# Differences of two SBUF operands on VectorE instead of GpSimd, and weight preparation begun earlier, in a kernel of attention and two feed-forward networks

## The chip, the cores and the metric

One Trainium2 chip, one core of it. The engines are TensorE (PE, with its weight loads as PEld), VectorE (DVE), ScalarE (ACT), GpSimd (POOL) and SyncE (SP, which here issues all transfers). The metric is the device time of one execution in microseconds, as the median of several runs.

## The reference

Causal attention in a window of 128 positions (4 sequences of 576, 8 heads of 64, with a linear position bias), then two feed-forward networks (FFN) over all 2304 tokens, everything in float32:

```python
x = attention(q, k, v)                    # 2304 x 512
h = x @ w_in                              # 512 -> 2048, first FFN
y = (h / (1 + exp(-1.702 * h))) @ w_out   # 2048 -> 512
g = y @ w_gate                            # 512 -> 1536, second FFN
out = (g / (1 + exp(-g)) * (y @ w_val)) @ w_out2
```

The weights come as float64 (pairs of 32-bit words), which the kernel turns into float32 itself.

## The kernel before

**Split operands.** Each operand of a large matmul is held as two parts, a high part that ScalarE copies (to type float32r) and a low part, the difference of the original and the high part. Each product is three matmuls: high x high, high x low, low x high (`three`, and the inner loops of `product` and `o_part`). The low parts are what the change is about: every one of them is a subtraction of two SBUF operands, or in some places of PSUM and SBUF.

**First FFN.** The 18 tiles of 128 tokens form five blocks of 4, 2, 4, 4, 4 tiles. `seq` is the order of 80 steps (block j, slice f of 16): the first eight slices of block 0, all of block 1, the second half of block 0, then blocks 2, 3, 4. A step is `h_part` (12 matmuls into `hp`; ScalarE's tanh; VectorE's `th`, L584; ScalarE's copy `gh`; VectorE's difference `gl`, L592) and `y_part` of the step two before (`AHEAD = 2`; 12 matmuls). The attention of blocks 0 and 1 and the first eight steps follow a handwritten list (`PLAN`). The attention of blocks 2 to 4 runs beside the steps of the block before: scores on TensorE, exponentials on ScalarE, and on GpSimd `normalise` (L421) and two selections (L478, L481).

**Preparation.** The generator `preparation` turns the second FFN's weights into what its products read and stores them in scratch memory (`w_scratch`, `wo_scratch`). There are 36 units: for each of six pairs of feature slices, two of the gate, two of the value and two of the output weights. A gate or value unit takes eight steps: a load (`raw`), three VectorE instructions of 512 columns beside one of ScalarE (`fraction`, L217, L219, L223), four sums and differences of 128 columns (L271), and three calls of `halves` (L229 copies, L230 subtracts: `wa` twice with 256 columns, `wb` with 384), with two stores. An output unit takes four steps, one subtraction of 512 columns and one store. Loads, stores and buffers turn over one unit at a time. `advance(n)` adds n to an account and takes as many steps as it holds, each inside `issue_after` for the two marks, the latest ScalarE and VectorE instructions of the main work: the instructions of the step are queued behind these on their engines. It is called twice in each step of the first FFN with a pace that depends on the block, and once after each product of the second FFN.

**Second FFN.** The tokens form three superblocks of six tiles. Each of 18 periods q (superblock s, pair p) has 14 products of 384 columns (`gv_steps`: seven for the gate and seven for the value, a form of 2 x 2 block multiplication with seven products in place of eight) and six products of 512 columns (`o_part`) that read the gated result `p` of the period before. The seven operands of a superblock are differences of quarters of y, loaded from scratch memory (`yr`): `y_steps` makes them in four stretches, with seven calls of `split` (L650 copies, L651 subtracts, 768 columns) and four of `minus` (L655, 768 columns). In `gate`, VectorE makes `th` (L725, L726), ScalarE copies the high part of `p` (L728) and L729 subtracts; VectorE's sums `c` (L716) free TensorE's accumulators.

**Order.** Outside `PLAN` the order of instructions on each queue comes from a schedule made at build time with a model of durations; the `issue_after` hints are edges in it. On the chip each engine, and SP's queue of transfers, keeps that order.

Of the kernel before, what the change touches and what calls it, by code (L numbers as in the profile page):

```python
# [8 lines left out]
F32 = mybir.dt.float32  # L9
# [4 lines left out]
ALU = mybir.AluOpType  # L14
# [8 lines left out]
F0 = 8  # L23

CLOSE = 6

PACE = {2: 1.8, 3: 1.8, 4: 3.4}

PAUSE = 13

PACE_LATE = 0.7

O_SLOTS = 4

# [47 lines left out]
def attention_two_ffn(ctx: ExitStack, tc: tile.TileContext, q, k, v, w_in, w_out, w_gate, w_val, w_out2, yscr, wscr, woscr, out):  # L82
# [5 lines left out]
    nc = tc.nc  # L88
# [5 lines left out]
    NF1 = w_in.shape[0]  # L94
# [27 lines left out]
    def bank(name):  # L122
        return ps.tile([P, 512], F32, tag="b", name=name)
# [103 lines left out]

    def halves(t, at, src):
        nc.scalar.activation(out=t[:, at, 0, :], in_=src, func=AF.Copy)  # L229
        nc.gpsimd.tensor_tensor(out=t[:, at, 1, :], in0=src, in1=t[:, at, 0, :].bitcast(F32), op=ALU.subtract)  # L230

    def flat(t):
        return t.bitcast(F32).rearrange("p s r c -> p (s r c)")
# [332 lines left out]
    marks = {}  # L566
# [71 lines left out]
    def y_steps(s, tile_of):  # L638

        t0 = s * SUPER * P  # L640

        def quarter(i, j):
            t = yrp.tile([P, 2, HT], F32, tag="yr", name="yr")
            a = t0 + j * HT
            nc.sync.dma_start(out=t, in_=yscr[:, 2 * i : 2 * i + 2, a : a + HT])
            return t

        def split(c, src):
            t = tile_of(c)
            nc.scalar.activation(out=t[:, 0], in_=src, func=AF.Copy)  # L650
            nc.gpsimd.tensor_tensor(out=t[:, 1], in0=src, in1=t[:, 0].bitcast(F32), op=ALU.subtract)  # L651
            y2[s, c] = t

        def minus(out_, a, b):
            (nc.gpsimd if s else nc.vector).tensor_tensor(out=out_, in0=a, in1=b, op=ALU.subtract)  # L655

        b11, b12, b22 = quarter(0, 0), quarter(0, 1), quarter(1, 1)
        split(1, b11)
        minus(b11, b12, b11)
        minus(b12, b22, b12)  # L660
        split(5, b11)
        yield
        minus(b11, b22, b11)
        split(7, b12)
        b21 = quarter(1, 0)
        yield
        split(2, b21)
        split(6, b11)
        yield
        split(3, b22)  # L670
        minus(b11, b21, b11)
        split(4, b11)
        yield
# [16 lines left out]
    def product(q, m, i, bank_, start):  # L690
        half, at = W_OF[i]
        w, y = w2[q, m, half], y2[q // NP2, i]
        for kk in range(2):
            for n, (a, b) in enumerate(((0, 0), (0, 1), (1, 0))):
                nc.tensor.matmul(  # L695
                    out=bank_[:, :HT],
                    lhsT=w[:, kk, at, a, :],
                    rhs=y[:, b, kk, :],
                    start=start and kk == 0 and n == 0,
                    stop=kk == 1 and n == 2,  # L700
                    skip_group_check=True,
                )

    def gv_steps(q):

        banks, kept, c = {}, {}, {}
        p2[q] = [wpool.tile([P, 2, 2 * HT], F32R, tag=f"w{12 + 2 * (q % 2) + f}", name="p2") for f in range(2)]

        def keep_copy(m, i, b):
            t = pp.tile([P, HT], F32, tag="pc", name="pc", bufs=5)  # L710
            marks["a"] = nc.scalar.activation(out=t, in_=b[:, :HT], func=AF.Copy).ins
            kept[m, i] = t

        def add(m, i, b, k):
            t = pp.tile([P, HT], F32, tag="c2", name="c2", bufs=4)
            marks["d"] = nc.vector.tensor_tensor(out=t, in0=b[:, :HT], in1=kept[m, k], op=ALU.add).ins  # L716
            c[m, i] = t

        def gate(i):
            f, j = i  # L720
            g, v = c["G", i], c["V", i]
            at = slice(j * HT, (j + 1) * HT)
            th = pp.tile([P, HT], F32, tag="th2", name="th2", bufs=3)
            nc.scalar.activation(out=th, in_=g, func=AF.Tanh, scale=0.5)
            nc.vector.scalar_tensor_tensor(out=th, in0=th, scalar=1.0, in1=g, op0=ALU.add, op1=ALU.mult)  # L725
            nc.vector.tensor_tensor(out=th, in0=th, in1=v, op=ALU.mult)  # L726
            ph = p2[q][f]
            nc.scalar.activation(out=ph[:, 0, at], in_=th, func=AF.Copy)  # L728
            nc.gpsimd.tensor_tensor(out=ph[:, 1, at], in0=th, in1=ph[:, 0, at].bitcast(F32), op=ALU.subtract)  # L729

        def step(m, i):
            b = {1: "x", 6: "x", 7: "x", 4: "x", 2: "y", 5: "z", 3: "z"}[i]
            new = (m, b) not in banks
            if new:
                banks[m, b] = bank("s" + b)
            t = banks[m, b]
            product(q, m, i, t, new)
            if i in (1, 5, 6):
                keep_copy(m, i, t)
            elif i == 2:  # L740
                add(m, (0, 0), t, 1)
            elif i == 3:
                add(m, (0, 1), t, 6)
            elif i == 7:
                add(m, (1, 1), t, 5)
            else:
                c[m, (1, 0)] = t[:, :HT]
            if m == "V" and i in (2, 3, 7, 4):
                gate({2: (0, 0), 3: (0, 1), 7: (1, 1), 4: (1, 0)}[i])

        for pair in ((1, 5), (2, 6), (3,), (7,), (4,)):
            for m in "GV":
                for i in pair:
                    step(m, i)
                    yield m, i
# [119 lines left out]
    na = len(a_blocks)  # L875
# [52 lines left out]
    def preparation():  # L928
        raws = []

        def fetch_next():
            if len(raws) < len(todo):
                raws.append(fetch(slot, todo[len(raws)]))

        fetch_next()
        yield
        for i, u in enumerate(todo):
            yield from prepare(slot, raws[i], fetch_next, u)

    work, owed = preparation(), [0.0]  # L940

    def advance(n):
        owed[0] += n
        while owed[0] >= 1:
            owed[0] -= 1
            with ExitStack() as after:
                for ins in marks.values():
                    after.enter_context(tc.issue_after(ins))
                next(work, None)

    for idx, (j, f) in enumerate(seq):
        if idx < F0:
            continue
        if (j, f) == (1, 0):
            load_w1(NW1)
        if j < 2:
            need = f + 2
            if j == 1:
                need = max(need, F0 + (NF1 - F0) * (f + 1) // NF1)
            split_next(w1, raw1, need)  # L960
        if (j, f) == (na - 1, CLOSE):
            closed.append(True)
            attx.close()
            ya = bctx.enter_context(tc.tile_pool(name="ya", bufs=1, side="right", reuse_waits="tile"))
            yrp = bctx.enter_context(tc.tile_pool(name="yrp", bufs=3, side="right", reuse_waits="tile"))
            first = y_steps(0, lambda c: ya.tile([P, 2, 2, HT], F32R, tag=f"ya{c}", name="ya"))
        h_part(j, f)
        run(2 * idx)
        if (j, f) < (na - 1, PAUSE):
            advance(PACE.get(j, 0))  # L970
        if idx >= AHEAD:
            y_part(*seq[idx - AHEAD])
        run(2 * idx + 1)
        if (j, f) < (na - 1, PAUSE):
            advance(PACE.get(j, 0))
        if j == na - 1 and f > CLOSE and f % 2:
            next(first, None)
    for i in range(len(seq) - AHEAD, len(seq)):
        y_part(*seq[i])
    for m, half in (("G", 0), ("V", 0), ("G", 1), ("V", 1), ("O", 0)):  # L980
# [6 lines left out]
    pieces = {}  # L987
    for q in range(NQ):
        s, p = divmod(q, NP2)
        if s + 1 < NS and p == NP2 - 2:  # L990
            pool, tag = ((wpool, "w"), (ya, "ya"))[s % 2]
            base = (0, 1)[s % 2]
            pieces[s + 1] = y_steps(
                s + 1,
                lambda c, pool=pool, tag=tag: pool.tile(
                    [P, 2, 2, HT], F32R, tag=f"w{c - 1}" if tag == "w" else f"ya{c}", name="ya"
                ),
            )
        for n, (m, i) in enumerate(gv_steps(q)):
            if q or n > 5:  # L1000
                advance(PACE_LATE)
            if q > 0 and n == 11:
                o_part(q - 1, O_ORDER[0])
            if s + 1 in pieces and n % 6 == 5:
                next(pieces[s + 1], None)
            if q + 1 < NQ and i in (6, 4):
                load_weights(q + 1, m, 0 if i == 6 else 1)
        if q == NQ - 2:
            load_weights(NQ - 1, "O", 0)
        if q > 0:  # L1010
            for i in O_ORDER[1:]:
                o_part(q - 1, i)
            if q < NQ - 1:
                load_weights(q, "O", 0)
# [46 lines left out]
```

## Time and profile before

| | |
|---|---|
| median of 3 runs | 949.06 us (946.11 to 949.38) |
| profiled execution | 945.89 us |
| its span, first to last instruction | 944.2 us |
| granted TensorE clock | 0.992 of full speed |
| busy: TensorE, weight loads | 919.8, 787.9 us |
| busy: VectorE, ScalarE, GpSimd | 598.2, 422.0, 333.8 us |

Busy times are sums over the span of instructions' durations, overlaps counted once. Matmuls are pipelined, so a busy TensorE can still be below its full pace. On the span's axis the first FFN runs to about 520 us (block 2 from 207, block 3 from 315, block 4 from 425) and the second FFN from there.

### The profile page before, as it was taken

The numbers are of one execution on the slowest core, as the hardware profiler recorded it, in microseconds if no ns is written. First come the engines' busy times: TensorE is split into PE (matmuls) and PEld (weight loads), VectorE is DVE, ScalarE is ACT, GpSimd is POOL, SyncE is SP. The second block draws the span as 40 slices with busy tenths as digits, with TensorE's granted clock in tenths as the row PEclk, the third lists the DMA queues.
The fourth block names the chain that finished last, engine by engine and source line by source line (L and its number), as shares of the span: only waits on it lengthen the run. The fifth ranks groups of instructions, "written<-read, shape, count | busy, mean of one in ns | idle before, by whom it ended". The sixth has DMA issues, their size and how long they took to land.

```text
span 944.2 us, 15242 instructions
## 1 busy us (share of the span) xinstructions
PE 919.8 (97%) x5464; PEld 787.9 (83%) x5464; DVE 598.2 (63%) x1373; ACT 422.0 (45%) x968; POOL 333.8 (35%) x406
## 2 busy tenths in 40 slices
PE   7899999999999999999999999999999999999998
PEld 5577898877778777788877899998999999999996
DVE  7897797536774666566587856756734545534555
ACT  5664566524563455434444554434342233243221
POOL 4734004403543344423364433369711111111211
PEclk8899999999999999999999999999999999999999
DMA  9963202304442443236659988867585566866641
GB/s 326 345 212 119 102 2 72 94 16 156 149 158 92 156 163 114 92 121 227 218 199 357 341 297 321 310 232 259 173 321 197 204 230 216 272 211 217 215 156 67
DMA packets 62476, 182.40 MB, mean 193 GB/s; under 512 B 6080, under 2 KB 28096, under 8 KB 55488
## 3 DMA queue, kind: packets, MB, share of 16 engines
q1 hardware_dynamic: 62400, 181.43, 54.6%
q8 instruction: 43, 0.70, 0.3%
q14 instruction: 33, 0.27, 0.1%
HBM read 142.61 MB, written 38.80 MB: 192 GB/s over the span
## 4 chain that ended last, share of the span: by engine, by line
PE 74%; DMA 9%; DVE 9%; POOL 3%; issue 2%; ACT 2%; SPq 0%; POOLq 0%; DVEq 0%; ACTq 0%
PE sx L695 13%; PE o L765 13%; PE sz L695 7%; PE hp L561 5%; PE hp L563 5%; PE hp L562 5%; PE y L563 5%; PE y L562 5%; PE y L561 5%; PE sy L695 3%; PE sb L361 2%; PE xb L514 2%; DMA wraw<-in_moe_w_out 2%; PE pt L453 2%; POOL ya L651 1%
## 5 line engine op out<-in xcount | busy, mean ns | idle before, releaser
L695 PE MATMUL sx<-ya,wg 128*128 128x384 f32 x864 | 173.7, 337 | 4.0 <-DMA wg<-w_scratch 2.1
L695 PEld LDWEIGHTS sx<-ya,wg 128*128 128x128 f32 x864 | 152.6, 188 | 11.6 <-DVE c L716 5.4
L729 POOL TENSOR_TENSOR p<-th,p 128x384 fp32r<-128x384 f32 x72 | 75.9, 1054 | 240.4 <-ACT p L728 115.9
L765 PE MATMUL o<-wo,p 128*128 128x512 f32 x648 | 159.7, 391 | 0.0
L765 PEld LDWEIGHTS o<-wo,p 128*128 128x128 f32 x648 | 120.7, 188 | 21.5 <-DVE c L716 0.2
L421 POOL TENSOR_SCALAR prob<-prob,stat 128x128 f32<-128x128 f32 x144 | 68.3, 492 | 157.9 <-DVE sb L331 55.6
L562 PE MATMUL y<-gl,wt 128*128 128x512 f32 (+1 forms) x320 | 117.5, 373 | 4.5 <-DVE gl L592 4.3
L561 PE MATMUL hp<-xh,wt 128*128 128x512 f32 (+1 forms) x320 | 121.0, 378 | 0.5 <-DVE th L584 0.4
L563 PE MATMUL hp<-xh,wt 128*128 128x512 f32 (+1 forms) x320 | 118.1, 370 | 0.0
L562 PE MATMUL hp<-xl,wt 128*128 128x512 f32 (+1 forms) x320 | 117.9, 369 | 0.0
L563 PE MATMUL y<-gh,wt 128*128 128x512 f32 (+1 forms) x320 | 117.1, 372 | 0.0
L561 PE MATMUL y<-gh,wt 128*128 128x512 f32 (+1 forms) x320 | 111.3, 377 | 0.1
L695 PE MATMUL sz<-ya,wg 128*128 128x384 f32 x432 | 84.1, 335 | 0.0
L774 DVE SCALAR_TENSOR_TENSOR acc<-o,acc 128x512 f32<-128x512 f32 x90 | 60.9, 687 | 34.7 <-PE o L765 33.3
L592 DVE TENSOR_TENSOR gl<-th,gh 128x512 fp32r<-128x512 f32 (+1 forms) x80 | 52.7, 663 | 42.8 <-ACT gh L590 42.2
L695 PEld LDWEIGHTS sz<-ya,wg 128*128 128x128 f32 x432 | 75.8, 188 | 0.2
L562 PEld LDWEIGHTS y<-gl,wt 128*128 128x128 f32 x320 | 60.4, 189 | 17.1 <-DVE gl L592 7.0
L590 ACT ACTIVATE gh<-th 128x512 fp32r<-128x512 f32 (+1 forms) x80 | 46.6, 585 | 62.6 <-PE y L563 42.9
L230 POOL TENSOR_TENSOR wa<-cs,wa 128x256 fp32r<-128x256 f32 x48 | 41.5, 872 | 93.5 <-ACT wa L229 88.9
L584 DVE SCALAR_TENSOR_TENSOR th<-th,hp 128x512 f32<-128x512 f32 (+1 forms) x80 | 49.8, 629 | 37.3 <-ACT th L582 36.6
L402 ACT ACTIVATE prob<-prob,stat 128x128 f32<-128x128 f32 x144 | 56.2, 393 | 36.9 <-DVE stat L386 36.7
L728 ACT ACTIVATE p<-th 128x384 fp32r<-128x384 f32 x72 | 37.5, 520 | 77.2 <-DVE th L726 77.2
(91 smaller groups left out, 1527.7 us busy)
## 6 DMA issues: line engine op xcount, KB each, us to landing
wg<-w_scratch SPq DMA_DIRECT2D x36, 1024.0 KB, 6.9
wg<-w_scratch SPq DMA_DIRECT2D x36, 768.0 KB, 5.4
wo<-wo_scratch SPq DMA_DIRECT2D x18, 1024.0 KB, 6.7
w_scratch<-wa SPq DMA_DIRECT2D x24, 512.0 KB, 3.0
w_scratch<-wb SPq DMA_DIRECT2D x24, 384.0 KB, 3.1
wraw<-in_moe_w_in SPq DMA_DIRECT2D x16, 512.0 KB, 7.8
wraw<-in_moe_w_out SPq DMA_DIRECT2D x16, 512.0 KB, 8.7
raw<-in_moe_w_gate SPq DMA_DIRECT2D x24, 256.0 KB, 3.6
```

The source lines that it names most:

```text
L402: nc.scalar.activation(out=prob[:, x], in_=prob[:, x], func=AF.Exp, bias=stat[:, 0, x : x + 1], scale=-1.0, accum_out=stat[:, 1, x : x + 1],)
L421: (nc.vector if (j, hp, g) in NORM_ON_VECTOR else nc.gpsimd).tensor_scalar(out=prob[:, x], in0=prob[:, x], scalar1=stat[:, 3, x : x + 1], ...
L561: nc.tensor.matmul(out=out_ap, lhsT=whi, rhs=xhi, start=start, stop=False)
L562: nc.tensor.matmul(out=out_ap, lhsT=whi, rhs=xlo, start=False, stop=False)
L563: nc.tensor.matmul(out=out_ap, lhsT=wlo, rhs=xhi, start=False, stop=stop)
L584: nc.vector.scalar_tensor_tensor(out=th[:, :m], in0=th[:, :m], scalar=1.0, in1=hp[:, :m], op0=ALU.add, op1=ALU.mult)
L590: a = nc.scalar.activation(out=gh[:, :m], in_=th[:, :m], func=AF.Copy)
L592: d = nc.vector.tensor_tensor(out=gl[:, :m], in0=th[:, :m], in1=gh[:, :m].bitcast(F32), op=ALU.subtract)
L695: nc.tensor.matmul(out=bank_[:, :HT], lhsT=w[:, kk, at, a, :], rhs=y[:, b, kk, :], start=start and kk == 0 and n == 0, stop=kk == 1 and n ...
L729: nc.gpsimd.tensor_tensor(out=ph[:, 1, at], in0=th, in1=ph[:, 0, at].bitcast(F32), op=ALU.subtract)
L765: nc.tensor.matmul(out=o, lhsT=ph[:, a, c], rhs=w[:, f, b, :], start=f == 0 and n == 0, stop=f == 1 and n == 2)
L774: nc.vector.scalar_tensor_tensor(out=acc, in0=o, scalar=0.5, in1=acc, op0=ALU.mult, op1=ALU.add)
```

## The change

Four places that subtract two SBUF operands on GpSimd do so on VectorE: `halves` (preparation), `split` and the differences `minus` of the second and third superblock (`y_steps`), and the low part of `p` in `gate`. Preparation's paces change, and it begins in block 0's second half (step 24 of 80) in place of block 2's start; it pauses at the same step as before, 77. The steps of the first superblock's differences come at f = 6, 8, 10 and so on of block 4 in place of 7, 9, 11, and they and the later superblocks' steps are traced inside `issue_after` for the marks, as preparation's were.

```diff
--- before.py
+++ after.py
@@ -24,11 +24,11 @@
 
 CLOSE = 6
 
-PACE = {2: 1.8, 3: 1.8, 4: 3.4}
-
-PAUSE = 13
-
-PACE_LATE = 0.7
+PACE = {0: 1.4, 2: 2.0, 3: 2.2, 4: 2.3}
+
+PAUSE = 77
+
+PACE_LATE = 0.6
 
 O_SLOTS = 4
 
@@ -227,7 +227,7 @@
 
     def halves(t, at, src):
         nc.scalar.activation(out=t[:, at, 0, :], in_=src, func=AF.Copy)
-        nc.gpsimd.tensor_tensor(out=t[:, at, 1, :], in0=src, in1=t[:, at, 0, :].bitcast(F32), op=ALU.subtract)
+        nc.vector.tensor_tensor(out=t[:, at, 1, :], in0=src, in1=t[:, at, 0, :].bitcast(F32), op=ALU.subtract)
 
     def flat(t):
         return t.bitcast(F32).rearrange("p s r c -> p (s r c)")
@@ -648,11 +648,11 @@
         def split(c, src):
             t = tile_of(c)
             nc.scalar.activation(out=t[:, 0], in_=src, func=AF.Copy)
-            nc.gpsimd.tensor_tensor(out=t[:, 1], in0=src, in1=t[:, 0].bitcast(F32), op=ALU.subtract)
+            nc.vector.tensor_tensor(out=t[:, 1], in0=src, in1=t[:, 0].bitcast(F32), op=ALU.subtract)
             y2[s, c] = t
 
         def minus(out_, a, b):
-            (nc.gpsimd if s else nc.vector).tensor_tensor(out=out_, in0=a, in1=b, op=ALU.subtract)
+            nc.vector.tensor_tensor(out=out_, in0=a, in1=b, op=ALU.subtract)
 
         b11, b12, b22 = quarter(0, 0), quarter(0, 1), quarter(1, 1)
         split(1, b11)
@@ -726,7 +726,7 @@
             nc.vector.tensor_tensor(out=th, in0=th, in1=v, op=ALU.mult)
             ph = p2[q][f]
             nc.scalar.activation(out=ph[:, 0, at], in_=th, func=AF.Copy)
-            nc.gpsimd.tensor_tensor(out=ph[:, 1, at], in0=th, in1=ph[:, 0, at].bitcast(F32), op=ALU.subtract)
+            nc.vector.tensor_tensor(out=ph[:, 1, at], in0=th, in1=ph[:, 0, at].bitcast(F32), op=ALU.subtract)
 
         def step(m, i):
             b = {1: "x", 6: "x", 7: "x", 4: "x", 2: "y", 5: "z", 3: "z"}[i]
@@ -939,14 +939,17 @@
 
     work, owed = preparation(), [0.0]
 
+    def in_order(steps):
+        with ExitStack() as after:
+            for ins in marks.values():
+                after.enter_context(tc.issue_after(ins))
+            return next(steps, None)
+
     def advance(n):
         owed[0] += n
         while owed[0] >= 1:
             owed[0] -= 1
-            with ExitStack() as after:
-                for ins in marks.values():
-                    after.enter_context(tc.issue_after(ins))
-                next(work, None)
+            in_order(work)
 
     for idx, (j, f) in enumerate(seq):
         if idx < F0:
@@ -966,15 +969,15 @@
             first = y_steps(0, lambda c: ya.tile([P, 2, 2, HT], F32R, tag=f"ya{c}", name="ya"))
         h_part(j, f)
         run(2 * idx)
-        if (j, f) < (na - 1, PAUSE):
-            advance(PACE.get(j, 0))
+        if F0 + NF1 <= idx < PAUSE:
+            advance(PACE[j])
         if idx >= AHEAD:
             y_part(*seq[idx - AHEAD])
         run(2 * idx + 1)
-        if (j, f) < (na - 1, PAUSE):
-            advance(PACE.get(j, 0))
-        if j == na - 1 and f > CLOSE and f % 2:
-            next(first, None)
+        if F0 + NF1 <= idx < PAUSE:
+            advance(PACE[j])
+        if j == na - 1 and f >= CLOSE and (f - CLOSE) % 2:
+            in_order(first)
     for i in range(len(seq) - AHEAD, len(seq)):
         y_part(*seq[i])
     for m, half in (("G", 0), ("V", 0), ("G", 1), ("V", 1), ("O", 0)):
@@ -1002,7 +1005,7 @@
             if q > 0 and n == 11:
                 o_part(q - 1, O_ORDER[0])
             if s + 1 in pieces and n % 6 == 5:
-                next(pieces[s + 1], None)
+                in_order(pieces[s + 1])
             if q + 1 < NQ and i in (6, 4):
                 load_weights(q + 1, m, 0 if i == 6 else 1)
         if q == NQ - 2:
```

## Rows read from the trace of the kernel before

**Rows 1.** The page: busy us (share) x instructions of each engine.

```profile
PE 919.8 (97%) x5464; PEld 787.9 (83%) x5464; DVE 598.2 (63%) x1373; ACT 422.0 (45%) x968; POOL 333.8 (35%) x406
```

**Rows 2.** Stages: stretch, length; PE, PEld, DVE, ACT, POOL busy (count); clock, DMA share, GB/s.

```profile
154.70:206.70 52.00, 52.00 (x462) 42.20 (x461) 26.87 (x100) 25.99 (x72) 17.06 (x36) 1.00 0.23 71
206.70:314.60 107.90, 107.90 (x738) 85.40 (x737) 68.52 (x213) 51.56 (x137) 41.09 (x66) 1.00 0.39 135
314.60:425.00 110.40, 110.40 (x738) 86.12 (x737) 69.24 (x210) 53.87 (x143) 45.22 (x69) 1.00 0.36 125
425.00:479.00 54.00, 54.00 (x240) 44.72 (x239) 33.09 (x62) 25.05 (x49) 17.45 (x20) 1.00 0.64 226
479.00:520.50 41.50, 37.48 (x159) 29.07 (x158) 34.61 (x45) 19.18 (x34) 24.15 (x17) 1.00 0.80 287
541.00:607.00 66.00, 66.00 (x350) 61.76 (x349) 44.95 (x77) 30.92 (x64) 22.65 (x21) 1.00 0.86 311
607.00:680.00 73.00, 71.15 (x368) 64.84 (x367) 47.27 (x60) 30.57 (x57) 55.99 (x35) 1.00 0.65 228
680.00:920.00 240.00, 240.00 (x1266) 224.74 (x1265) 112.10 (x199) 79.10 (x162) 42.96 (x43) 1.00 0.64 225
```

**Rows 3.** Slices of 10 us and one of 50; columns as in rows 2.

```profile
160.00:170.00 10.00, 10.00 (x134) 8.05 (x129) 7.95 (x36) 7.67 (x25) 3.86 (x8) 1.00 0.42 133
340.00:350.00 10.00, 10.00 (x59) 7.80 (x58) 8.22 (x38) 5.75 (x19) 6.32 (x9) 1.00 0.15 58
480.00:490.00 10.00, 8.19 (x36) 6.48 (x36) 9.96 (x10) 3.91 (x7) 7.25 (x5) 1.00 0.49 185
750.00:800.00 50.00, 50.00 (x266) 46.94 (x265) 23.11 (x41) 15.43 (x32) 8.11 (x8) 1.00 0.68 233
```

**Rows 4.** Waits of TensorE, 480 to 541 and 640 to 680: us, times, longest.

```profile
PEld y L562 <- DVE gl L592: 6.1, 5, 2.2
...
PE sx L695 <- DMA wg<-w_scratch: 2.1, 1, 2.1
...
PEld sx L695 <- DVE c L716: 3.0, 3, 1.8
```

**Rows 5.** VectorE in order of time, 476 to 520: start, us, instruction.

```profile
481.44 2.22 DVE L219 SCALAR_TENSOR_TENSOR raw<-raw 128x512 uint32<-128x512 uint32 x1
...
491.46 0.95 DVE L655 TENSOR_TENSOR yr<-yr 128x768 f32<-128x768 f32 x1
...
507.23 0.43 DVE L217 TENSOR_SCALAR raw<-raw 128x512 uint32<-128x512 uint32 x1 [0.90 <-ACT cs L216]
507.69 0.69 DVE L219 SCALAR_TENSOR_TENSOR raw<-raw 128x512 uint32<-128x512 uint32 x1
```

**Rows 6.** GpSimd in order of time, the same stretch.

```profile
478.84 4.27 POOL L651 TENSOR_TENSOR ya<-yr,ya 128x768 fp32r<-128x768 f32 x2
```

**Rows 7.** Stages, L651 on GpSimd alone: stretch, length, busy (count).

```profile
607.00:680.00 73.00, 26.43 (x14) 1.00 0.65 228
```

**Rows 8.** Groups by line: busy us, mean ns of one; idle before.

```profile
L729 POOL TENSOR_TENSOR p<-th,p 128x384 fp32r<-128x384 f32 x72 | 75.9, 1054 | 240.4 <-ACT p L728 115.9 <-PE sz L695 106.4 <-issue 18.0
...
L230 POOL TENSOR_TENSOR wa<-cs,wa 128x256 fp32r<-128x256 f32 x48 | 41.5, 872 | 93.5 <-ACT wa L229 88.9 <-DVE sb L331 4.4
...
L651 POOL TENSOR_TENSOR ya<-yr,ya 128x768 fp32r<-128x768 f32 x21 | 40.9, 1957 | 11.7 <-ACT ya L650 10.8 <-DMA yr<-y_scratch 1.0
...
L271 DVE TENSOR_TENSOR cs<-cs 128x128 f32<-128x128 f32 x96 | 38.4, 432 | 0.8
...
L230 POOL TENSOR_TENSOR wb<-cs,wb 128x384 fp32r<-128x384 f32 x24 | 25.5, 1061 | 6.5 <-ACT wb L229 5.6 <-POOL wa L230 0.8
...
L230 POOL TENSOR_TENSOR wo<-cs,wo 128x512 fp32r<-128x512 f32 x12 | 15.5, 1294 | 49.0 <-ACT wo L229 36.7 <-PE sz L695 4.6 <-PE sy L695 3.9
```

**Rows 9.** SP's queue in order of time, 526 to 534: issue of transfers.

```profile
529.76 1.56 SPq L632 DMA_DIRECT2D y_scratch<-yt  x2
...
531.41 0.59 SPq L684 DMA_DIRECT2D wg<-w_scratch  x1
```

## Prediction, made before the changed kernel ran

> **What bounds the kernel now.** Start with the page's table of engines [rows 1]: TensorE shows work in 97% of the span, no other engine in more than 63%. So time can only go where TensorE stands still or runs below its pace, and the next view, busy time by stage, says where that is [rows 2]. Take the columns of TensorE and VectorE, with the matmul counts in brackets. From 680 to 920 us (late second FFN) TensorE is busy for all 240 us; nothing that another engine does faster can shorten that. The stages from 155 to 479 us (attention and first FFN) are full as well. Two are not: 479 to 520.5 (end of the first FFN) with 37.48 of 41.5, and 607 to 680 with 71.15 of 73. Matmul ends are modelled, so I also count matmuls. From 425 to 479, 240 of them took 54 us, 0.225 each; the 159 of the next stage are then worth 35.8 of its 41.5 us, a loss of 5.7 where idle time alone gives 4.0. In the steady second FFN 266 took 50 us, 0.188 each [rows 3]; the 368 of 607 to 680 are worth 69.2 of 73, a loss of 3.8 against 1.85. I take 5.0 and 3.5.
>
> The list of waits, cut to the stretches around these losses, names the causes [rows 4]: at the end of the first FFN weight loads into the array wait for `gl` (VectorE, L592), and once TensorE waits 2.1 us for a transfer of `wg`; later, weight loads wait for VectorE's sum `c` (L716). With the 2.1 there are 5.0 + 2.1 + 3.5 = 10.6 us to be had, between bounds of 4.0 + 2.1 + 1.85 = 8.0 and 5.7 + 2.1 + 3.8 = 11.6.
>
> Why VectorE is late there stands in its order of time [rows 5]. One 128x512 fraction step (L219) takes 2.22 us at 481 us and 0.69 us at 508. The slow one falls into the 4.27 us in which GpSimd does two subtractions of L651 [rows 6]: while GpSimd works on SBUF operands, VectorE's instructions on SBUF stretch threefold. In 480 to 490 us VectorE is busy for 9.96 us of 10 and TensorE loses 1.81 [rows 3]. The second loss is of the same kind: 14 of the 21 subtractions of L651 run from 607 to 680 [rows 7]. By the code seven of these (for the third superblock) belong to periods 10 and 11, some 100 us later; nothing held them back on GpSimd's queue.
>
> **The change, part by part.** *Subtractions.* GpSimd loses five groups of 41.5, 25.5, 15.5, 40.9 and 75.9 us [rows 8], and L655's eight differences, at L651's price for the same size 8 x 1.957 = 15.7: 215 us. VectorE gains the same 185 instructions. Its price for two SBUF operands is 0.69 for 512 columns and 0.95 for 768 (L655) [rows 5], so by the line through these two 0.43 for 256 and 0.56 for 384. That makes 48 x 0.43 + 24 x 0.56 + 12 x 0.69 + 72 x 0.56 + 29 x 0.95 = 110 us, half of GpSimd's. Where VectorE has room these microseconds cost TensorE nothing, so what counts is each stage's load, and against it stands the stretching that ends.
>
> *Preparation's pace.* The 36 units have 24 x 8 + 12 x 4 steps, 241 with the first load. Before: 2 x 16 x 1.8 twice, then 2 x 13 x 3.4, that is 203 of them by step 77, and the other 38 at 0.7 a product. After: 22 beside block 0's second half, 64, 70 and 60 beside blocks 2, 3 and 4, so 216, and the other 25 at 0.6. Each unit's load from memory, its stores of `wa`, `wb` or `wo` and its turn of buffers move with its steps, on SP's queue. Block 4 gets 4.6 steps in each of its 5.4 us (24 matmuls) in place of 6.8. A gate or value unit of 8 steps costs VectorE 0.43 + 0.69 + 0.69 (its third 512-column step has the second's form) [rows 5], 4 x 0.43 at most [rows 8], and 2 x 0.43 + 0.56 for the subtractions: 5.0 us, 0.62 a step, of which 0.18 is new.
>
> *VectorE's load by stage after*, from rows 2 and with no stretching taken off: block 0's second half 26.9 + 22 x 0.62 = 40.5 of 52 us (78%); block 2 68.5 + 64 x 0.18 + 6 more steps x 0.44 = 82.7 of 108; block 3 69.2 + 70 x 0.18 + 13 x 0.44 = 87.5 of 110 (79%). Block 4 to 479 us is best built anew: `th` and `gl` of 0.69 in each of ten steps, 46 x 0.62, and six of the second FFN's first differences, 13.8 + 28.5 + 5.7 = 48 of 54 (89%), the fullest. The rest of the first FFN has six steps, 14 of preparation and five differences, 8 + 9 + 5 = 22 of 37. From 541 to 607 us it is 45 + 13 x 0.56 + 8 x 0.5 = 56 of 66 (85%). From 607 to 680 the steady rate, 23.11 in 50 [rows 3], gives 33.7; with 12 x 0.56 + 11 x 0.95 that is 51 of 73, where 47.3 stood before. No stage comes near the 9.96 of 10 that cost TensorE 1.81.
>
> Within a step the queue matters too: behind a subtraction that waits for ScalarE's copy stand `th`, `gl` and `c`. The hints of `issue_after` put preparation's and the differences' work behind the latest of these, and y follows its h by two steps, 10.8 us, which covers a wait of that kind; without that cover it costs about one instruction, 0.7 us, each time. In the gate, the product that reads `p` comes eleven products after the last gate, with the same effect.
>
> *Differences for the second FFN.* The first superblock's start one step earlier (f = 6, 8, 10, 12), behind the marks, and the third's stay in periods 10 and 11. A period there is 22.9 us with VectorE busy for 10.6; 4 x 0.56 and 5.2 more keep it under 80%.
>
> *The weight wait.* That load of `wg` was issued at 531.41 us, behind the last stores of `y` on SP's queue [rows 9], where preparation's transfers stand too. A third less preparation in block 4 shortens the queue and the transfer; the stores of `y` stay. I count 1.5 of 2.1, between none and all.
>
> **Sum.** Of 5.0, 2.1 and 3.5 I take 4.0, 1.5 and 3.3 as gone, 8.8 us. Against it I set 0.5 for block 0's second half, where 7.95 of 10 us at 160 [rows 3] plus 4.3 steps x 0.62 passes 10. The bounds of that are nothing (the two steps' cover hides it) and 1.8 in each of two slices, 3.6. The profiled execution took 945.89 us (span 944.2 and 1.7 around it), so it would give 937.6. The median of the runs shown, 949.06, lies 3.2 above it; from there the same 8.3 gives **940.8 us**. All gone and no new loss is 949.06 - 11.6 = 937.5, and a median nearer to the profiled run takes it to 935.
>
> **Rivals.** *The stall at the end of the first FFN stays (0.18).* The first superblock's buffers open when preparation has left its own. Asked for a step earlier, with preparation slower, their loads may stand on SP's queue until then, and VectorE, whose queue is in order, waits on them with `gl` behind. For it: this is VectorE's fullest stage after the change. Against it: the cover of 10.8 us. Only 3.3 and half a microsecond of the weight wait are won: 945.3 us.
>
> *VectorE becomes the bound (0.10), slower.* If attention's bursts and 0.18 to 0.62 us more for each step fill it for whole slices, TensorE loses 1.8 us in each that reaches 9.9 of 10. To be slower the rival needs more than (8.8 + 4.7) / 1.8, eight of the 25 slices between 155 and 405 us. For it: 8.22 of 10 at 340 us, 7.95 at 160 [rows 3]. Against it: in blocks 2 and 3 a slice gains about 1.4, so 9.6 at most. With eleven such slices: 949.06 - 8.8 + 19.8 = 960 us. The Trainium skill (Perfetto Trace Analysis, Optimizing Scalar/DVE Operations) speaks for this rival: when VectorE is saturated, moving work off it, even to GpSimd, may make sense, and this change goes the opposite way; by that rule the time would be the 960. The same passage warns that the two share an SBUF read port, so that such a move might not help; the stretched row agrees with the warning.
>
> *The change does what it says and nothing is won (0.10).* What is won is given back in small pieces, by another order of instructions after block 0 or weight loads that come late again: 947 to 951 us.
>
> **Chances.** About 0.5%, 4.7 us, is what a measurement can tell from no change here. The forecast has 0.62 (936.5 to 944), the rivals 0.18, 0.10 and 0.10. Faster is the forecast and a little of the first rival, 0.65; within 0.5% its rest and nearly all of the third, 0.25; slower 0.10. The range, 935 to 949.5, takes in the first rival and most of the third and leaves out about 0.15.
>
> **What would show it.** In the profile after, L230, L651, L655 and L729 stand under VectorE near 0.43 to 0.95 us by size; L217 and L219 have no values of 1.8 and 2.2; weight loads wait less than 2 us for `gl` and `c` after 479 us; L651 runs in three separate groups, the last near 740 to 790 us; VectorE's share rises from 63% to about 70%. The forecast is wrong if TensorE falls below 99% of a stage between 155 and 479 us, if `gl` still holds it at the end of the first FFN, or if `wg` lands as late as before.

## The result and the profile after

The changed kernel takes 938.65 us in the median of six runs (936.9 to 940.68), the kernel before 949.16 beside it; the ratio is 0.9892 with a 95% interval of 0.9874 to 0.9911. That is faster by 10.5 us, 1.1%, inside the range and 2.2 us under the forecast of 940.8. The profiled execution took 937.2 us against 945.89, a span of 935.4. The two profiled executions thus lie 8.7 us apart and the medians 10.5; the traces can account for the 8.7 alone.

The page's table of engines after, which answers to [rows 1]:

```profile
PE 916.7 (98%) x5464; PEld 788.6 (84%) x5464; DVE 649.0 (69%) x1558; ACT 422.0 (45%) x968; POOL 123.6 (13%) x221
```

GpSimd's busy time falls by 210 us, VectorE's rises by only 50.8. The stages, with the columns of [rows 2]; the limits follow the same events:

```profile
155.30:207.70 52.40, 52.24 (x463) 42.11 (x461) 35.47 (x122) 29.76 (x81) 18.02 (x36) 1.00 0.38 125
207.70:318.30 110.60, 110.43 (x738) 86.89 (x736) 78.89 (x243) 52.89 (x144) 26.19 (x48) 1.00 0.45 153
318.30:427.70 109.40, 109.40 (x738) 85.75 (x737) 78.71 (x244) 55.56 (x147) 24.80 (x48) 1.00 0.43 150
427.70:479.00 51.30, 51.30 (x228) 42.49 (x227) 38.30 (x78) 24.53 (x47) 0.00 (x0) 1.00 0.64 226
479.00:520.00 41.00, 41.00 (x185) 34.24 (x184) 26.46 (x50) 16.19 (x29) 0.00 (x0) 1.00 0.71 250
...
541.00:607.00 66.00, 66.00 (x349) 61.62 (x348) 45.50 (x86) 28.38 (x57) 0.00 (x0) 1.00 0.82 296
607.00:680.00 73.00, 73.00 (x388) 68.56 (x386) 49.65 (x87) 27.60 (x53) 0.00 (x0) 1.00 0.69 244
680.00:920.00 240.00, 240.00 (x1260) 224.13 (x1260) 142.72 (x255) 83.88 (x166) 0.00 (x0) 1.00 0.60 210
```

From 479 to 520 us TensorE is now busy without a gap, 185 matmuls in 41 us where 159 stood in 41.5, and from 607 to 680 it does 388 in place of 368. VectorE is nowhere over 75% of a stage. The slice at the end of the first FFN and the second FFN's steady stretch (now with the third superblock's differences in it), which answer to those of [rows 3]:

```profile
480.00:490.00 10.00, 10.00 (x45) 8.26 (x44) 8.77 (x18) 4.45 (x9) 0.00 (x0) 1.00 0.65 222
750.00:800.00 50.00, 50.00 (x265) 46.77 (x264) 37.71 (x67) 20.41 (x38) 0.00 (x0) 1.00 0.68 248
```

VectorE does have slices without any gap, where the second FFN's differences are made, and TensorE is at work through all of them, with 51 or 52 matmuls where the steady stretch has 53:

```profile
611.00:621.00 10.00, 10.00 (x52) 9.11 (x51) 10.00 (x17) 3.74 (x8) 0.00 (x0) 1.00 0.52 199
749.00:759.00 10.00, 10.00 (x51) 8.96 (x51) 10.00 (x17) 4.18 (x7) 0.00 (x0) 1.00 0.54 200
```

Weight loads into the array at the end of the first FFN; where [rows 4] had 6.1 us for `gl`, this one row is the whole list, and TensorE's own list of waits there is empty:

```profile
PEld sx L695 <- issue: 0.3, 1, 0.3
```

The subtractions under VectorE, by line, beside lines that VectorE had before too (columns of [rows 8]):

```profile
L729 DVE TENSOR_TENSOR p<-th,p 128x384 fp32r<-128x384 f32 x72 | 39.9, 554 | 15.4 <-ACT p L728 15.4
...
L726 DVE TENSOR_TENSOR th<-th,c 128x384 f32<-128x384 f32 x54 | 29.8, 552 | 0.5
...
L271 DVE TENSOR_TENSOR cs<-cs 128x128 f32<-128x128 f32 x96 | 26.2, 302 | 0.8
...
L219 DVE SCALAR_TENSOR_TENSOR raw<-raw 128x512 uint32<-128x512 uint32 x36 | 25.2, 701 | 0.4
...
L651 DVE TENSOR_TENSOR ya<-yr,ya 128x768 fp32r<-128x768 f32 x21 | 19.9, 952 | 0.0
...
L230 DVE TENSOR_TENSOR wa<-cs,wa 128x256 fp32r<-128x256 f32 x48 | 19.4, 431 | 0.8 <-ACT wa L229 0.8
```

L729 takes 554 ns in place of GpSimd's 1054, L651 952 in place of 1957. L271, whose mean was 432 ns, is down to 302. No L219 takes more than 1.12 us, where the slow one of [rows 5] took 2.22. L726 before:

```profile
L726 DVE TENSOR_TENSOR th<-th,c 128x384 f32<-128x384 f32 x54 | 39.1, 724 | 0.7
```

L651 by stretch (busy time and count behind the comma), which answers to [rows 7]:

```profile
470.00:520.00 50.00, 6.59 (x7) 1.00 0.74 264
...
600.00:650.00 50.00, 6.65 (x7) 1.00 0.68 237
...
740.00:790.00 50.00, 6.66 (x7) 1.00 0.67 242
```

Seven for each superblock, the last seven some 100 us later than before. SP's queue at the start of the second FFN, as in [rows 9]:

```profile
521.46 1.80 SPq L632 DMA_DIRECT2D y_scratch<-yt  x4
527.64 1.88 SPq L684 DMA_DIRECT2D wg<-w_scratch  x2
```

The first `wg` load of period 1 is issued 3.8 us earlier than before on the span's axis, and no wait for it shows. Counted from the first product of period 0 (520.6 us before, 517.4 after) it is only 0.6 us earlier; the rest comes from the shorter stage ahead of it. It lands 5.1 us after its issue, in place of 6.6.

**Where the time went, stage by stage.** Busy time alone hides losses, so I compare lengths between the same events: the starts of block stages (first `hp` matmul of the step) and of periods (every 84th product matmul), in TensorE's order of time. "Start" is the time up to step 24, whose order is mostly the handwritten list's; it varies between 154.4 and 156.4 us in all runs without a pattern.

| profile | start | block 0, 2nd half | block 2 | block 3 | block 4 to period 2 | periods 2 to 7 | rest |
|---|---|---|---|---|---|---|---|
| before | 154.7 | 52.0 | 107.9 | 110.4 | 138.3 | 117.1 | 263.8 |
| after | 155.3 | 52.4 | 110.6 | 109.4 | 130.1 | 114.1 | 263.6 |
| difference | 0.6 | 0.4 | 2.7 | -1.0 | -8.2 | -3.0 | -0.2 |

The two losses of the forecast returned 11.2 us, more than the 8.8 that were taken. Block 2 gave 2.7 back, where the forecast had nothing. The stage from block 4 to period 2 holds both the wait for `gl` and the wait for the weights. The first product of period 0 parts them: up to it the stage fell from 95.6 to 89.8 us, and behind it (periods 0 and 1) from 42.7 to 40.3.

### The profile page after: what moved, and what is told of

Its sections match the earlier page's. It is cut to its first block, busy times and chain, and to the rows that moved or that the text cites. A ratio compares the mean times of both kernels' runs of the same rounds, so it can differ in the third digit from the quotient of the medians.

```text
span 935.4 us, 15014 instructions
## 1 busy us (share of the span) xinstructions
PE 916.7 (98%) x5464; PEld 788.6 (84%) x5464; DVE 649.0 (69%) x1558; ACT 422.0 (45%) x968; POOL 123.6 (13%) x221
## 4 chain that ended last, share of the span: by engine, by line
PE 86%; DVE 6%; DMA 3%; ACT 2%; POOL 1%; issue 1%; SPq 0%; DVEq 0%; POOLq 0%; ACTq 0%
PE sx L695 16%; PE o L765 16%; PE sz L695 8%; PE hp L561 6%; PE y L561 6%; PE hp L563 6%; PE y L563 6%; PE hp L562 6%; PE y L562 6%; PE sy L695 4%; PE xb L514 2%; PE sb L361 2%; PE pt L453 1%; DMA y_scratch<-yt 1%; DVE wraw L194 1%; POOL prob L421 1%
## 5 line engine op out<-in xcount | busy, mean ns | idle before, releaser
L561 PE MATMUL y<-gh,wt 128*128 128x512 f32 (+1 forms) x320 | 111.2, 377 | 0.2 <-DVE stat L386 0.2
L592 DVE TENSOR_TENSOR gl<-th,gh 128x512 fp32r<-128x512 f32 (+1 forms) x80 | 52.4, 659 | 44.7 <-ACT gh L590 44.3
L716 DVE TENSOR_TENSOR c<-sy,pc 128x384 f32<-128x384 f32 x36 | 20.1, 558 | 79.5 <-PE sy L695 75.3
L561 PEld LDWEIGHTS hp<-xh,wt 128*128 128x128 f32 x320 | 60.4, 189 | 13.6 <-issue 1.6
L563 PEld LDWEIGHTS y<-gh,wt 128*128 128x128 f32 x320 | 60.3, 188 | 11.2 <-issue 1.0
L563 PEld LDWEIGHTS hp<-xh,wt 128*128 128x128 f32 x320 | 60.2, 188 | 10.6
```

The source lines that it names most:

```text
L561: nc.tensor.matmul(out=out_ap, lhsT=whi, rhs=xhi, start=start, stop=False)
L563: nc.tensor.matmul(out=out_ap, lhsT=wlo, rhs=xhi, start=False, stop=stop)
L592: d = nc.vector.tensor_tensor(out=gl[:, :m], in0=th[:, :m], in1=gh[:, :m].bitcast(F32), op=ALU.subtract)
```

## The experiments

Theory A is the prediction's: GpSimd's reads of SBUF stretch VectorE's instructions, so moving the subtractions removes the stalls. Theory B: the new paces and the hints do it, whatever the engine. Stage lengths are read as above, from one profile of each run; ratios are to the kernel before in the same comparison.

| kernel | median us | ratio (95%) | block 0 | block 2 | block 3 | block 4 to period 2 | periods 2 to 7 |
|---|---|---|---|---|---|---|---|
| e1: before, subtractions moved | 939.42 | 0.9899 (0.9882 to 0.9915) | 52.0 | 108.5 | 109.6 | 134.1 | 114.2 |
| e2: after, subtractions back | 939.39 | 0.9906 (0.9889 to 0.9924) | 53.0 | 110.6 | 109.8 | 131.4 | 114.1 |
| e3: before, differences of y moved | 942.10 | 0.9930 (0.9914 to 0.9946) | 52.0 | 107.9 | 110.4 | 137.0 | 114.1 |
| e4: after, start at block 2 | 937.85 | 0.9885 (0.9870 to 0.9899) | 52.0 | 110.1 | 110.3 | 130.5 | 114.1 |
| e5: before, hints added | 944.26 | 0.9967 (0.9955 to 0.9979) | 52.0 | 107.9 | 110.4 | 140.1 | 114.1 |
| e6: before, subtractions moved, other paces | 934.71 | 0.9871 (0.9855 to 0.9888) | 52.0 | 108.5 | 108.8 | 130.2 | 114.1 |
| e7: after, the same other paces | 934.28 | 0.9866 (0.9851 to 0.9880) | 52.0 | 108.5 | 108.8 | 130.6 | 114.1 |
| e8: after, block 2 at 1.8 | 941.68 | 0.9945 (0.9930 to 0.9959) | 52.5 | 109.5 | 114.2 | 130.8 | 114.1 |
| e9: after, unaltered | 938.22 | 0.9903 (0.9885 to 0.9921) | 52.5 | 111.0 | 109.9 | 130.5 | 114.1 |
| e10: after, differences of y back | 938.69 | 0.9903 (0.9879 to 0.9928) | 52.4 | 111.2 | 109.4 | 130.6 | 114.1 |
| e11: before, other paces alone | 941.72 | 0.9933 (0.9909 to 0.9957) | 52.0 | 107.9 | 110.0 | 134.3 | 116.7 |
| e12: e6 again | 934.56 | 0.9868 (0.9848 to 0.9888) | 52.0 | 108.5 | 108.8 | 133.9 | 114.1 |

Up to period 0's first product the stage from block 4 takes 89.8 us in every kernel of this table but e2 (90.8), e5 (94.0) and e11 (91.9); before it took 95.6. Behind it, in periods 0 and 1, lie 40.3 us (after) to 47.2 (e3). e6 and e12 are the same kernel, and 3.7 us lie between their profiles in this second part, so one profile says little about it.

**Each half of the change alone (e1, e2).** e1 edits the kernel before in four lines:

```diff
-        nc.gpsimd.tensor_tensor(out=t[:, at, 1, :], in0=src, ...)
+        nc.vector.tensor_tensor(out=t[:, at, 1, :], in0=src, ...)
-            nc.gpsimd.tensor_tensor(out=t[:, 1], in0=src, ...)
+            nc.vector.tensor_tensor(out=t[:, 1], in0=src, ...)
-            (nc.gpsimd if s else nc.vector).tensor_tensor(out=out_, ...)
+            nc.vector.tensor_tensor(out=out_, ...)
-            nc.gpsimd.tensor_tensor(out=ph[:, 1, at], in0=th, ...)
+            nc.vector.tensor_tensor(out=ph[:, 1, at], in0=th, ...)
```

> The kernel before with all four subtractions on VectorE, its paces and order left as they were. Theory A (GpSimd's reads stretch VectorE's instructions, so the engine of the subtractions decides): the waits for gl and c after 479 us mostly go, 940 to 944 us; not all, since 6.8 preparation steps of 0.62 us and 1.4 us of th and gl ask for 5.6 us of VectorE in each 5.4 us step of block 4. Theory B (the paces and the hints decide): 947 to 951 us, with the stall at the end of the first FFN in place.

e2 takes the same four lines of the changed kernel back:

```diff
-        nc.vector.tensor_tensor(out=t[:, at, 1, :], in0=src, ...)
+        nc.gpsimd.tensor_tensor(out=t[:, at, 1, :], in0=src, ...)
...
-            nc.vector.tensor_tensor(out=ph[:, 1, at], in0=th, ...)
+            nc.gpsimd.tensor_tensor(out=ph[:, 1, at], in0=th, ...)
```

> The changed kernel (new paces, early start, hints) with the four subtractions back on GpSimd. Theory A: 947 to 951 us, single VectorE instructions of 1.8 us and more remain while L651 runs. Theory B: 938 to 942 us.

Both gave nearly the whole gain, 939.4 us each; neither theory expected that of both. In e2 VectorE's instructions are still stretched, as Theory A said. GpSimd in order of time, and VectorE at the same moment:

```profile
501.60 3.91 POOL L651 TENSOR_TENSOR ya<-yr,ya 128x768 fp32r<-128x768 f32 x2 [2.12 <-ACT ya L650]
```

```profile
503.38 0.42 DVE L217 TENSOR_SCALAR raw<-raw 128x512 uint32<-128x512 uint32 x1
503.84 2.22 DVE L219 SCALAR_TENSOR_TENSOR raw<-raw 128x512 uint32<-128x512 uint32 x1
```

L219 again takes 2.22 us while L651 runs. Not every instruction is stretched: L217 just before it, beside L651 too, took 0.42. But weight loads waited only this for `gl` from 480 to 541 us, against 6.1:

```profile
PEld y L562 <- DVE gl L592: 1.2, 2, 0.9
```

So the stretching is real, and it stalls TensorE only where something else has used up the slack.

**Which half of the half (e3, e5).** e3 moves only L651 and L655 in the kernel before:

```diff
-            nc.gpsimd.tensor_tensor(out=t[:, 1], in0=src, ...)
+            nc.vector.tensor_tensor(out=t[:, 1], in0=src, ...)
-            (nc.gpsimd if s else nc.vector).tensor_tensor(out=out_, ...)
+            nc.vector.tensor_tensor(out=out_, ...)
```

> The kernel before with only the second FFN's differences (L651, L655; 29 instructions of 768 columns) on VectorE. Theory A in its narrow form (the long L651 and L655 alone cause both stalls): 940 to 943 us, nearly the whole gain. If the short subtractions of 256 to 512 columns stretch VectorE as much: 945 to 948 us.

942.1 us, inside the first range, though only two thirds of the gain (0.9930 against 0.9892). The wait for `gl` nearly ends. The stage of periods 2 to 7 is down to 114.1, although 14 subtractions of L651 still run from 607 to 680 us, now on VectorE:

```profile
607.00:680.00 73.00, 15.08 (x14) 1.00 0.75 262
```

But at the start of the second FFN, where the shorter subtractions are still GpSimd's, weight loads wait for `c`, and the stage from block 4 keeps 137.0 us:

```profile
PEld sx L695 <- DVE c L716: 2.7, 1, 2.7
...
PEld y L562 <- DVE gl L592: 0.7, 1, 0.7
```

e5 adds only the hints to the kernel before:

```diff
-            next(first, None)
+            in_order(first)
...
-                next(pieces[s + 1], None)
+                in_order(pieces[s + 1])
```

> The kernel before with only the hints on the second FFN's differences; paces and GpSimd's subtractions stay. Read by stage (before: 138.3 us from block 4's start to period 2, 117.1 from period 2 to 7). If the hints cure the second loss, the stage from period 2 to 7 falls to 114.1 and the third superblock's differences run in periods 10 and 11; 945 to 946 us. If they also cure the stall at the end of the first FFN, the stage before falls under 134 and the time to 941 to 943. If the stretching needs the other engine, nothing changes: 948 to 950.

The first outcome: periods 2 to 7 take 114.1, the stall at the end of the first FFN stays. Its wait for `gl`, and then L651 on GpSimd by stretch:

```profile
PEld y L562 <- DVE gl L592: 3.7, 2, 2.9
```

```profile
600.00:650.00 50.00, 10.91 (x6) 1.00 0.74 260
650.00:740.00 90.00, 2.40 (x2) 1.00 0.70 240
740.00:790.00 50.00, 11.96 (x6) 1.00 0.63 221
```

An instruction across a limit counts on both sides: the second superblock's seven run before 740 us and the third's after it, all still on GpSimd at some 1.9 us each, and the stage loses nothing. The second loss therefore needed both superblocks' differences in one stretch on GpSimd. Holding them apart cures it (e2, e5), and so does VectorE (e1, e3).

**The rate of preparation (e11, e6, e10).** e11 changes only numbers of the kernel before:

```diff
-PACE = {2: 1.8, 3: 1.8, 4: 3.4}
+PACE = {2: 1.8, 3: 2.4, 4: 2.3}
-PACE_LATE = 0.7
+PACE_LATE = 0.8
```

> The kernel before with only the paces 1.8, 2.4, 2.3 and 0.8: GpSimd's subtractions, no hints on the differences, no early start. If the pace alone cures the stall and the weight wait: 130.5 to 132 us from block 4 to period 2, 117 from period 2 to 7, near 941 us. If the engine is needed: 135 us or more, 945 to 947.

941.72 us, with 134.3 and 116.7: the time is near the first expectation's, the first stage lies between the two. The slower rate shortens the wait for `gl` from 6.1 to 2.6 us without ending it, and the second loss stays, with both superblocks' differences on GpSimd in one stretch. Weight loads and then TensorE itself (its row for `wg`), 480 to 541 us:

```profile
PEld y L562 <- DVE gl L592: 2.6, 3, 1.3
PEld sx L695 <- DVE c L716: 2.4, 1, 2.4
```

```profile
PE sx L695 <- DMA wg<-w_scratch: 2.1, 1, 2.1
```

The last two rows are one stop, and the weights end it: the last `c` before it is done at 534.78 us, the transfer of `wg` lands at 534.96, and the matmul starts at 535.09.

e10 puts L651 and L655 of the changed kernel back on GpSimd and keeps the rest:

```diff
-            nc.vector.tensor_tensor(out=t[:, 1], in0=src, ...)
+            nc.gpsimd.tensor_tensor(out=t[:, 1], in0=src, ...)
-            nc.vector.tensor_tensor(out=out_, ...)
+            (nc.gpsimd if s else nc.vector).tensor_tensor(out=out_, ...)
```

> The changed kernel with only the second FFN's differences (L651, L655) back on GpSimd. If GpSimd's long reads alone make the stall at the end of the first FFN, it comes back: the stage from block 4 is 134 us or more, 942 us. If the stall also needs preparation at 6.8 steps in each step of block 4, as the run with new paces and GpSimd's subtractions suggests (131.4), the stage is 130 to 132 us and the time 938 to 940.

130.6 and 114.1: no stall, as the second expectation had it. So the first stall, too, needed two things at once: GpSimd's long reads, and the old order around them, that is preparation at 6.8 steps for each step of block 4 and differences without hints. Without the long reads (e1 and e3), or with the slower rate and the hints together (e2 and e10), `gl` waits 1.2 us or less. The slower rate alone (e11) leaves 2.6 us and the hints alone (e5) 3.7. e2 and e10 also start preparation earlier; no run tells that apart here. An edit of the engine also moves the order that the build-time schedule makes: of TensorE's 396 matmuls from block 4's start to period 0, 12 stand at another place in e3 and 6 in e1. So e1 and e3 show engine and order together. What ties the stall to the stretching is VectorE's order of time in the kernel before, ahead of the wait of 2.2 us for `gl` that ends at 489.7:

```profile
485.65 2.50 DVE L655 TENSOR_TENSOR yr<-yr 128x768 f32<-128x768 f32 x1
488.07 1.01 DVE L271 TENSOR_TENSOR cs<-cs 128x128 f32<-128x128 f32 x2
489.01 0.68 DVE L592 TENSOR_TENSOR gl<-th,gh 128x512 fp32r<-128x512 f32 x1
```

L655 takes 2.50 us there and 0.95 at 491.46 [rows 5], and `gl` stands behind it.

**The weight wait.** e1 has no wait for `gl` from 480 us on, yet 134.1 us from block 4 to period 2. What TensorE waited for most there:

```profile
PE sx L695 <- DMA wg<-w_scratch: 1.9, 1, 1.9
```

At block 4's old pace every profile but e3 has 1.8 to 2.1 us of this wait (before, e1, e5; in e3 the wait for `c` came first). e6 joins e1's four lines with e11's numbers:

> The kernel before with all four subtractions on VectorE and other paces: 1.8, 2.4 and 2.3 for blocks 2, 3 and 4, 0.8 in the second FFN; no start beside block 0, no hints on the differences. If the 4 us that subtractions alone left in block 4 (134.1 against 130.1) are the weight transfer behind preparation's traffic at pace 3.4, that stage falls to 130 to 131; if it is VectorE's load, to 133 or more. Block 2 at pace 1.8 should keep its 108 to 108.5 us. 935 to 937 us by the first, 938 to 940 by the second.

130.2 and 108.5, and 934.71 us: the first outcome. At a pace of 2.3 the wait is 0 to 0.7 us in seven of nine other profiles, but 2.1 in e11 and 2.3 in the one profile of e12. A lower rate makes the wait rarer; it does not exclude it. In all ten profiles at 2.3 the load is issued 10.2 us after period 0's first product. Where it lands 5.1 us after its issue (after, e2, e6) TensorE doesn't wait for it; where it takes 7.1 us (e11) or 7.3 (e12) TensorE waits 2.1 and 2.3. So the wait follows the length of the transfer, and what lengthens it in e12 and not in e6, the same kernel, the runs don't show.

**Block 2 (e4, e7, e8, e9).** e4 and the two that follow change the changed kernel's paces:

```diff
-PACE = {0: 1.4, 2: 2.0, 3: 2.2, 4: 2.3}
+PACE = {0: 0.0, 2: 2.35, 3: 2.55, 4: 2.3}
```

> The changed kernel with preparation begun at block 2 again and its 22 steps spread over blocks 2 and 3 (paces 2.35 and 2.55), so that 216 steps are done by step 77 as before. If the 2.7 us lost in block 2 in the changed kernel's profile are VectorE's load, block 2 and 3 get slower still: 940 to 943 us. If they come from the start beside block 0: 935 to 938 us. If neither, the same as the changed kernel, 938 to 939 us.

937.85, and block 2 keeps its loss, 110.1: it isn't the start beside block 0. Nor is it the engine: e2 has 110.6 with the subtractions on GpSimd.

```diff
-PACE = {0: 1.4, 2: 2.0, 3: 2.2, 4: 2.3}
+PACE = {0: 0.0, 2: 1.8, 3: 2.4, 4: 2.3}
-PACE_LATE = 0.6
+PACE_LATE = 0.8
```

> The changed kernel with those same paces (none beside block 0, 1.8, 2.4, 2.3, late 0.8). If the pace in block 2 costs the 2.7 us there, the stage is 108 to 108.5 us and the time 935 to 937; if it is the order that the hints make, 110 us or more and 938 to 939.

108.5 and 934.28 us: the paces, not the hints. 0.6 of the 2.7 us remain in e1, e6 and e7 alike, and e1's edit is the subtractions' engine alone; the other 2.1 came with the paces. But e8 takes only block 2's pace back and keeps the early start:

```diff
-PACE = {0: 1.4, 2: 2.0, 3: 2.2, 4: 2.3}
+PACE = {0: 1.4, 2: 1.8, 3: 2.2, 4: 2.3}
```

> The changed kernel with only block 2's pace back at 1.8, the start beside block 0 kept. If block 2's pace costs the 2.7 us: 108 to 108.5 us there, 935.5 to 937 in all. If the early start costs them by what it leaves in flight: 110 us and 938 to 939.

941.68, a miss for both: 109.5 in block 2 and 4.8 us more in block 3, whose own pace was not touched. There TensorE waits for `th`, 1.8 us in all, where no other kernel of the table waits more than 0.4 in block 3:

```profile
PE hp L561 <- DVE th L584: 1.8, 2, 1.0
```

TensorE's value products in block 2 (L514, busy time and count behind the comma) show part of what moves. One row each for before, after and e2:

```profile
206.70:314.60 107.90, 7.39 (x192) 1.00 0.39 135
```

```profile
207.70:318.30 110.60, 9.72 (x192) 1.00 0.45 153
```

```profile
207.90:318.50 110.60, 8.20 (x192) 1.00 0.44 151
```

The same 192 matmuls take 2.3 us more in the changed kernel, nearly its whole loss there, but only 0.8 more in e2, whose loss is as large. A shifted preparation moves the attention's order around it, and the cost shows at different lines. The traces have this order: of TensorE's 736 matmuls in block 2, compared place by place by line and output, 14 differ from the kernel before in e1, e6 and e7, and 42 (e2) to 112 (after) in the kernels that lose over a microsecond there. That the order makes the loss is argued, not shown. Which shift costs and which doesn't stays open; so does e8's block 3.

**A faster version.** e9 is the changed kernel and e12 is e6, timed together.

> The changed kernel unaltered, beside the next three on one chip: 938 to 939.5 us, and the stages of its first profile (110.6, 109.4, 130.1, 114.1).

> The version of subtractions on VectorE, paces 1.8, 2.4, 2.3 and 0.8, no hints, no early start, again, timed on the chip that also runs the changed kernel: 934 to 935 us, 0.4% under the changed kernel.

938.22 and 934.56 us: moving the subtractions with paces 1.8, 2.4, 2.3 and 0.8, and neither early start nor hints, is 0.4% faster than the changed kernel (934.56 / 938.22 = 0.996) and 1.3% faster than the one before. e7, the same with the hints, gave 934.28 beside e6's 934.71, so no gain from them shows once VectorE subtracts.

## Why the prediction was right, point by point

- *TensorE bounds the kernel and loses in two places*: right. Both are full after the change, and the rest of the second FFN did not move (263.8 to 263.6).
- *10.6 us to be had, 8.8 of it gone*: the two places returned 11.2 us, 8.2 and 3.0, near the upper bound of 11.6. The terms of the first place, 4.0 + 1.5, were too small by 2.7: the part with the `gl` stall gave 5.8 and periods 0 and 1 gave 2.3, together more than the bound of 5.7 + 2.1. The one of the second, 3.3, was right. Against 2.4 us more of gain stands the 2.7 of block 2, which the sum left out; that 937.6 us for the profiled execution came within 0.4 of the 937.2 measured is in part luck.
- *The cause of VectorE's lateness*: right as a mechanism and incomplete as an explanation. The stretched instructions are there in every kernel whose long subtractions stay on GpSimd, but e2 wins 0.94% with them in place. Each stall needed a second condition (preparation's rate without the hints; two superblocks' differences at once), and the change removes both conditions of each.
- *The price on VectorE*: 110 us forecast. Measured for the 185 moved instructions: 39.9 + 19.9 + 19.4 by the rows above, 13.5 and 8.2 for L230's `wb` and `wo`, and eight of L655 at 0.952, 108.5. VectorE's busy time rose by 50.8. Of the other 58 us, some 42 are stretching that ended, by the busy time of each line before and after: 12.2 in L271, 9.3 in L726, 8.5 in L725, 5.1 in L217, 4.9 in L219 and 1.9 in the four of L655 that VectorE had before. The rest is mostly overlap of neighbouring instructions, which busy time counts once. The sum had left both out, on the safe side: block 4 to 479 us, put at 48 of 54 us (89%), has 38.30 of 51.3.
- *0.5 us in block 0's second half*: 0.4, and nothing in e4, e6 and e7, which do not start there. The reason given, a VectorE slice past 10 us, did not occur: the slice from 160 us has 7.92 after the change and the fullest behind it 8.11, so here the number was right by luck.
- *Blocks 2 and 3 are hidden*: the step that failed. Block 2 lost 2.7, and a share of 99% busy, which the prediction had named as its test, did not show it (110.43 of 110.6): TensorE was at work at a lower pace. 0.6 of it came with the subtractions, the rest with the new paces. Block 3 gained 1.0.
- *The first superblock's differences a step earlier*: wrong, here and in the description of the change. The new condition `(f - CLOSE) % 2` holds at odd f, since `CLOSE` is 6, so the steps are 7, 9, 11 and so on as before. The first of these subtractions does start earlier, 46.4 us into block 4 in place of 53.8, but e6, with the old condition and the new rate in block 4, has 46.1.
- *The rivals*: the stall at the end of the first FFN did not stay, and the earlier request on which this rival rested was not made. VectorE did not become the bound: no stage is over 75%. The price of 1.8 us for each slice that reaches 9.9 of 10 was wrong: from 611 and from 749 us VectorE is busy for 10.00 of 10 and TensorE too. A full VectorE cost TensorE time where its instructions were stretched ahead of `gl`. The third came true in small part, since block 2 gave 2.7 of the 11.2 back.
- *What would show it*: three groups of L651, the last from 749 us; VectorE at 69%; no L217 over 0.73 us and no L219 over 1.12; no wait for `gl` or `c` from 480 to 680 us; `wg` landing sooner. All as stated.

## What to carry to other kernels

When two engines' instructions stretch each other, ask what else must hold for the stall to reach the bounding engine; here removing either condition was enough, and two different halves of one change each gave nearly the whole gain. Compare lengths between the same events as well as busy shares, since TensorE was busy for 99.8% of block 2 and lost 2.7 us in it. Before pricing a full engine, check whether anything waits for it. And after moving work to a faster engine, try its paces again: some 4 us more lay in four numbers.

## What the runs showed of the hardware that was not expected

A stall can cost more than its length. In e1 TensorE stood nearly still from 533 to 535 us for the weights, and then the granted clock fell (columns of [rows 2], clock third from the end):

```profile
533.00:535.00 2.00, 0.34 (x2) 0.02 (x1) 2.00 (x5) 0.92 (x2) 0.00 (x0) 1.00 1.03 434
535.00:536.00 1.00, 0.71 (x2) 0.72 (x3) 1.00 (x3) 0.00 (x0) 0.00 (x0) 0.53 0.91 381
536.00:537.00 1.00, 1.00 (x4) 1.00 (x4) 0.12 (x1) 0.00 (x0) 0.00 (x0) 0.50 1.04 420
537.00:538.00 1.00, 1.00 (x4) 1.00 (x4) 0.00 (x0) 0.39 (x2) 0.00 (x0) 0.50 1.18 391
538.00:539.00 1.00, 1.00 (x6) 1.00 (x6) 0.46 (x1) 0.51 (x2) 0.00 (x0) 0.77 0.84 209
539.00:540.00 1.00, 1.00 (x8) 1.00 (x7) 0.10 (x1) 0.88 (x2) 0.00 (x0) 1.00 1.02 346
```

From 535 to past 538 us the clock is at half, 1.2 GHz in place of 2.4, and a microsecond holds four matmuls where it holds eight at 539. Waits of 0.4 and 1.9 us and 1.7 us lost at the low clock (from the clock column) make the 4.0 by which the stage is longer (134.1 against 130.1). e3, e5 and e12 have such a stretch too, after waits of 2.4, 2.4 and 2.3 us. The kernel before stood for 2.1 us at the same place and kept its clock, as did e11:

```profile
535.00:538.00 3.00, 1.08 (x7) 0.76 (x5) 3.00 (x7) 1.47 (x4) 2.16 (x3) 1.00 1.02 408
538.00:539.00 1.00, 0.81 (x5) 0.84 (x6) 0.84 (x3) 0.33 (x1) 1.00 (x2) 1.00 1.10 340
```

So a stall of some two microseconds does or does not draw the low clock; what decides it the runs don't show. In the profiles of the kernel before and the changed one the clock stays at 1.00 from block 2 to period 7, so it has no part in the 8.2 us that the stage gave.
